# Spectral block on one core: the weights' conversion put behind the first sequence's frequency stage, rows of the forward stage asked for one chunk ahead

## Chip, cores, metric

The kernel runs on one core of one Trainium2 chip. The metric is the device time of one execution in microseconds.

## What is computed

For a batch of 8 sequences of 3136 rows of 256 numbers (float32; the two MLP matrices come as float64):

```
X  = rfft(x, axis=1)                       # along the 3136 rows
Yr = X.real @ w_r - X.imag @ w_i + b_r
Yi = X.real @ w_i + X.imag @ w_r + b_i
Yr, Yi = sign(.) * max(|.| - 0.01, 0)      # soft threshold
y  = irfft(Yr + i Yi, n=3136, axis=1)
mixed = real(fft(fft(y, axis=1), axis=2))
u  = y + mixed
un = (u - mean(u)) / sqrt(var(u) + 1e-6)   # over the 256 numbers of a row
out = u + max(un @ w_ch1, 0) @ w_ch2       # 256 -> 1024 -> 256
```

## The kernel before

The transform of length 3136 is split as 64 x 49. Each sequence b goes through stages, each a generator:

- `p1` (forward, f1): loads 12 or 13 chunks of x (`xf`), multiplies with the DFT of 64 (`g_f1`), copies the result out of PSUM (`ev`, in turn by VectorE and ScalarE, L366) and stores it in DRAM (`ad`). From b = 2 on, x is first divided into a high part `xh` (ScalarE) and a low part `xl` (GpSimd).
- `p2_f2` (frequency transform, `g_f2` from `af` and the table `tff`, L419), `p2_w` (complex weights, bias, threshold: `g_w`, `Y`), `p2_mix` (`g_mix`, `mq`, stored in DRAM as `md`), `p2_yt` and `p2_g2` (inverse, `g_g2`, stored as `bd`). The frequencies come in four quarters q.
- `p3_norm`: per norm tile of 128 rows x 2 it loads `bf` from `bd` and `mt` from `md`, makes `bh` (ScalarE) and `bl` (GpSimd, L147), multiplies (`g_g1`), adds `mt` (`ut`, L683), takes mean and variance, a square root on ScalarE, four small products on GpSimd (L695 to L698) and writes the normalised tile `nm` (L701). `p3_tr` transposes `nm` (`g_ut`, L719), `p3_mlp1` and `p3_mlp2` are the MLP (`h`, `o`).

`weights()` turns w1 and w2 from float64 (read as pairs of int32) into a high and a low float32 matrix, in 8 parts, `split_double` (L158). A part is one load of 512 KB (`raw`), one operation on ScalarE (L169), seven on VectorE (L170, L172, L174, L175, L178, L180, L182), one copy on ScalarE (L186, the high matrix) and a subtraction and an addition on GpSimd (L188, L189, the low matrix). It borrows its tiles from other stages: `raw` has the two slots of `uth`, its scratch the two slots of `mt` and the six of `ut`. In the trace its tiles are called `raw_w`, `cv_w_mt` and `cv_w_ut`.

What sets the order: each generator yields due times, `yield T * x` with T = 10000 for one sequence's worth of work; a heap takes the generator that is due first, and the instructions it writes go out in that order. Then a scheduler of the framework, which works with its own estimate of times, puts each engine's instructions in their final order. Each engine executes its own in order. All loads and stores are asked for on SyncE's queue, in order too: a request that waits holds those behind it. A tile with n slots makes the n+1st writer wait for the last reader of the first. The first sequence's frequency stage is due from 1.0 to about 1.52, sequence 1's forward stage from 1.4, the frequency stage of sequence 1 from 1.77.

Of the kernel before, what the change touches and what calls it, by code (L numbers as in the profile page):

```python
# [10 lines left out]
F32 = mybir.dt.float32  # L11
# [8 lines left out]
D = 256  # L20
# [99 lines left out]
T = 10000  # L120
# [8 lines left out]
def spectral_block(ctx: ExitStack, tc: tile.TileContext, x, w_ri, b_ri, w1, w2,  # L129
# [6 lines left out]
    sb = ctx.enter_context(tc.tile_pool(name="sb", bufs=1))  # L136
# [3 lines left out]
    def gtile(name):  # L140
        return ps.tile([128, 512], F32, tag="g", bufs=4, name=name)
# [4 lines left out]
    def lo_g(out_, full, hi):  # L146
        gp.tensor_sub(out_, full, hi.bitcast(F32))  # L147

    def mm3(o, lh, ll, rh, rl, start=True, stop=True):
        te.matmul(o, lh, rl, start=start, stop=False)  # L150
        te.matmul(o, ll, rh, start=False, stop=False)  # L151
        return te.matmul(o, lh, rh, start=False, stop=stop)  # L152
# [105 lines left out]
    def behind(key, **kw):  # L258

        assert key in af_ld  # L260
        with tc.issue_after(af_ld[key]):
            return nc.sync.dma_start(**kw)
# [7 lines left out]
    def n2_rows(t, n0, n):  # L270

        return t[n0:n0 + n].rearrange("n c u d -> (c u) n d")

    def x_rows(b, m, n):

        if m == NM - 1:
            return [xv[b + r][:, m:m + 1] for r in range(2)]
        return [xv[b][:, NM * r + m:NM * r + m + n] for r in range(2)]
# [60 lines left out]
    def p1(b):  # L339

        if b == 0:
            yield from p1_first()
            return
        for i in (b, b + 1)[:1 + (b % 2 == 0)]:
            if i not in a_dram:
                ad = dr.tile([N2, 2, U, D], F32, tag="ad", bufs=4, name=f"ad{i}")
                a_dram[i] = lambda u, ad=ad: (ad, u)
        todo = chunks + [(NM - 1, 1)] * (b % 2 == 0)
        t0, width = (1.4, 0.38) if b == 1 else (b - 0.3, 0.75)
        for ci, (m, n) in enumerate(todo):  # L350
            yield T * (t0 + width * ci / len(todo))
            w = n * D
            xf = sb.tile([128, 512], F32, tag="xf", bufs=2, name="xf")
            for r, src in enumerate(x_rows(b, m, n)):
                behind(7, out=xf[r * 64:r * 64 + 64, :w], in_=src)
            g = gtile("g_f1")
            if b == 1:
                te.matmul(g[:, :w], fwd_f, xf[:, :w], start=True, stop=True)
            else:
                xh = sb.tile([128, 512], F32R, tag="xh", bufs=1, name="xh")  # L360
                xl = sb.tile([128, 512], F32R, tag="xl", bufs=1, name="xl")
                sc.copy(xh[:, :w], xf[:, :w])  # L362
                lo_g(xl[:, :w], xf[:, :w], xh[:, :w])
                mm3(g[:, :w], *K["fwd"], xh[:, :w], xl[:, :w])
            ev = sb.tile([128, 512], F32, tag="ev", bufs=2, name="ev")
            (va.tensor_copy if ci % 2 else sc.copy)(ev[:, :w], g[:, :w])  # L366
            for r in range(2):
                ad, n2 = (a_dram[b + r](0)[0], m) if n == 1 else (a_dram[b](0)[0], NM * r + m)
                st_eng.dma_start(out=n2_rows(ad, n2, n),
                                 in_=ev[r * 64:r * 64 + 64, :w].rearrange("p (n d) -> p n d", d=D))  # L370
        done.add(("a", b))
# [390 lines left out]
    def weights():  # L762
        w1v = w1.bitcast(I32).rearrange("(k p) f -> p k f", p=128)
        w2v = w2.bitcast(I32).rearrange("(f p) e -> p f e", p=128)
        parts1 = [(np.s_[:, k, q * 512:q * 512 + 512], w1v[:, k:k + 1, q * 1024:q * 1024 + 1024])
                  for k in range(2) for q in range(2)]
        parts2 = [(np.s_[:, f:f + 2, :], w2v[:, f:f + 2]) for f in range(0, 8, 2)]
        for i, (name, shape, loads) in enumerate((("w1", [128, 2, FF], parts1), ("w2", [128, 8, D], parts2))):
            h = sb.tile(shape, F32R, tag=f"W{2 * i}", bufs=1, name=name + "h")
            l = sb.tile(shape, F32R, tag=f"W{2 * i + 1}", bufs=1, name=name + "l")  # L770
            mlp_w[name] = h, l
            for j, (sl, src) in enumerate(loads):
                yield T * (1.2 + 0.5 * (4 * i + j) / 8)
                split_double(name, h, l, sl, src)


    tasks = [load_small(), load_consts(), weights()]
    for b in range(NB):
        tasks += [f(b) for f in (p1, p2_f2, p2_w, p2_mix, p2_yt, p2_g2, p3_norm, p3_tr, p3_mlp1, p3_mlp2)]
# [44 lines left out]
```

## Time and profile before

| | |
|---|---|
| median of 3 runs | 1957.9 us (1957.82 to 1959.0) |
| profiled execution | 1958.73 us, its span 1956.9 us |
| mean granted clock of TensorE | 0.973 |
| busy share of the span | TensorE 95%, VectorE 68%, ScalarE 43%, GpSimd 36% |
| chain that ended last | TensorE 80%, DMA 6%, VectorE 6% |

PE is TensorE, DVE VectorE, ACT ScalarE, POOL GpSimd, SPq the requests on SyncE's queue. Times count from the start of the span. An engine's idle time costs something only where it is on the chain that ends last. A granted clock of 0.50 is the lower of TensorE's two levels (1.2 GHz), 1.00 the upper (2.4 GHz).

### The profile page before, as it was taken

How to read it: one execution, taken by the hardware profiler on the slowest of the kernel's cores; microseconds unless marked ns; L12 is line 12 of the kernel's file. 1: busy time of each engine (PE TensorE's matmuls, PEld its weight loads, DVE VectorE, ACT ScalarE, POOL GpSimd, SP SyncE). 2: the span in 40 equal slices, each digit the busy share in tenths (PEclk: the TensorE clock that was granted, in tenths of full speed). 3: DMA queues.
4: the chain of work that ended last, by engine and by line, in shares of the span. 5: the costliest groups of instructions: out<-in, count | busy, mean ns of one | idle time of the engine just before them, and what ended most of it. 6: DMA issues, size and time to landing. Idle time of an engine off the chain costs nothing.

```text
span 1956.9 us, 34768 instructions
## 1 busy us (share of the span) xinstructions
PE 1853.1 (95%) x12115; PEld 1703.2 (87%) x12115; DVE 1327.2 (68%) x2831; ACT 851.0 (43%) x1888; POOL 702.1 (36%) x1087
## 2 busy tenths in 40 slices
PE   4875799999999999999999999999999999999999
PEld 2764699989999999998999899998999998998999
DVE  2675687768776777766677676666777776675543
ACT  2543554445444554443544454444544434433322
POOL 0334544344333444333433442324433332322110
PEclk7986899999999999999999999999999999999999
DMA  7466554245443544335453354535443332223210
GB/s 215 123 185 193 153 137 136 90 111 142 119 133 98 157 128 123 107 102 147 132 140 105 103 153 111 139 94 153 124 118 103 94 113 87 81 70 114 63 41 25
DMA packets 163538, 233.03 MB, mean 119 GB/s; under 512 B 27484, under 2 KB 107428, under 8 KB 163364
## 3 DMA queue, kind: packets, MB, share of 16 engines
q1 hardware_dynamic: 163364, 230.82, 42.1%
q8 instruction: 96, 1.57, 0.3%
q14 instruction: 78, 0.64, 0.1%
HBM read 127.95 MB, written 102.76 MB: 118 GB/s over the span
## 4 chain that ended last, share of the span: by engine, by line
PE 80%; DMA 6%; DVE 6%; SPq 3%; issue 2%; ACT 1%; POOL 1%; DVEq 0%; POOLq 0%; ACTq 0%
PE o L151 8%; PE o L150 8%; PE o L152 8%; PE h L150 8%; PE h L152 8%; PE h L151 8%; PE g_f L419 4%; PE g_w L150 3%; PE g_w L152 3%; PE g_w L151 3%; PE g_g L150 2%; PE g_g L152 2%; PE g_g L151 2%; PE g_yt L609 2%; PE g_ut L719 2%
## 5 line engine op out<-in xcount | busy, mean ns | idle before, releaser
L151 PE MATMUL o<-w2h,hl 128*128 128x256 f32 x1568 | 431.4, 285 | 9.1 <-DVE hl L739 9.1
L739 DVE SCALAR_TENSOR_TENSOR hl<-h,hh 128x512 fp32r<-128x512 f32 (+1 forms) x416 | 272.2, 655 | 238.1 <-ACT hh L738 237.4
L738 ACT ACTIVATE hh<-h 128x512 fp32r<-128x512 f32 (+1 forms) x416 | 237.7, 572 | 435.2 <-PE h L152 379.7
L152 PE MATMUL o<-w2h,hh 128*128 128x256 f32 x1568 | 423.5, 280 | 0.0
L150 PE MATMUL o<-w2l,hh 128*128 128x256 f32 x1568 | 397.3, 286 | 5.4 <-DVE ut L758 3.5
L150 PE MATMUL h<-utl,w1h 128*128 128x512 f32 (+1 forms) x832 | 323.0, 388 | 5.8 <-DVE hl L739 5.8
L152 PE MATMUL h<-uth,w1h 128*128 128x512 f32 (+1 forms) x832 | 316.8, 381 | 0.0
L151 PE MATMUL h<-uth,w1l 128*128 128x512 f32 (+1 forms) x832 | 316.3, 380 | 0.0
L151 PEld LDWEIGHTS o<-w2h,hl 128*128 128x128 f32 x1568 | 296.5, 189 | 16.6 <-DVE hl L739 12.2
L150 PEld LDWEIGHTS o<-w2l,hh 128*128 128x128 f32 x1568 | 285.3, 189 | 18.7 <-ACT Xsh L428 3.3
L152 PEld LDWEIGHTS o<-w2h,hh 128*128 128x128 f32 x1568 | 296.5, 189 | 3.1
L147 POOL TENSOR_TENSOR bl<-bf,bh 128x512 fp32r<-128x512 f32 x104 | 129.7, 1249 | 307.4 <-ACT bh L678 304.0
L419 PE MATMUL g_f<-tff,af 98*128 98x100 f32 x1024 | 154.5, 282 | 25.6 <-DMA tff<-c_tf 12.4
L152 PEld LDWEIGHTS h<-uth,w1h 128*128 128x128 f32 x832 | 156.6, 188 | 23.8
L419 PEld LDWEIGHTS g_f<-tff,af 98*128 98x128 f32 x1024 | 147.4, 203 | 34.2 <-issue 22.7
L150 PEld LDWEIGHTS h<-utl,w1h 128*128 128x128 f32 x832 | 156.9, 189 | 20.5 <-DVE hl L739 6.6
L151 PEld LDWEIGHTS h<-uth,w1l 128*128 128x128 f32 x832 | 157.0, 189 | 13.4
L147 POOL TENSOR_TENSOR xl<-xf,xh 128x512 fp32r<-128x512 f32 (+1 forms) x75 | 97.0, 1293 | 198.9 <-ACT xh L362 197.7
L683 DVE TENSOR_TENSOR ut<-g_g,mt 128x512 f32<-128x512 f32 x104 | 68.3, 657 | 107.1 <-PE g_g L152 71.9
L147 POOL TENSOR_TENSOR Xl<-xx,Xh 128x400 fp32r<-128x400 f32 (+1 forms) x96 | 106.5, 1111 | 91.7 <-ACT Xh L428 70.5
L147 POOL TENSOR_TENSOR Xsl<-xs,Xsh 128x200 fp32r<-128x200 f32 x120 | 77.5, 647 | 155.1 <-ACT Xsh L428 140.6
L701 DVE TENSOR_SCALAR nm<-ut,ag,rs 128x256 f32<-128x256 f32 x196 | 88.6, 491 | 48.1 <-POOL rs L698 47.7
(155 smaller groups left out, 3810.5 us busy)
## 6 DMA issues: line engine op xcount, KB each, us to landing
bd<-bev SPq DMA_DIRECT2D x128, 196.0 KB
af<-ad SPq DMA_DIRECT2D x62, 392.0 KB
bf<-bd SPq DMA_DIRECT2D x184, 128.0 KB
out_dram<-ut SPq DMA_DIRECT2D x92, 256.0 KB
xf<-in_x SPq DMA_DIRECT2D x176, 128.0 KB
ad<-ev SPq DMA_DIRECT2D x168, 128.0 KB
md<-mq SPq DMA_DIRECT2D x112, 192.0 KB
mt<-md SPq DMA_DIRECT2D x416, 32.0 KB
```

What stands on the lines that cost most here:

```text
L147: gp.tensor_sub(out_, full, hi.bitcast(F32))
L150: te.matmul(o, lh, rl, start=start, stop=False)
L151: te.matmul(o, ll, rh, start=False, stop=False)
L152: return te.matmul(o, lh, rh, start=False, stop=stop)
L419: te.matmul(g[:, o:o + 100], afs[s][:, ui * D + k * 128:ui * D + k * 128 + 128], tfs[s][:, ui], start=True, stop=True)
L609: te.transpose(gt[:100, (v * 2 + o) * 128:(v * 2 + o + 1) * 128], y[:, o, place].rearrange("p c j -> p (c j)"), ident)
L683: va.tensor_add(ut[:, :n], g[:, :w].rearrange("p (n d) -> p n d", d=D), mt[:, :n])
L701: va.tensor_scalar(nm[:, j], ut[:, j], ag[:, j, 0:1], rs[:, j], op0=ALU.subtract, op1=ALU.mult)
L719: te.transpose(gv[:, k, j * 128:(j + 1) * 128], nm[:, j, k * 128:(k + 1) * 128], ident)
L738: sc.activation(hh[:, :w], h[:, :w], AF.Relu)
L739: va.scalar_tensor_tensor(hl[:, :w], h[:, :w], 0.0, hh[:, :w].bitcast(F32), op0=ALU.max, op1=ALU.subtract)
```

## The change

Three edits. The loads of a forward chunk are written out at the due time of the chunk before it (`load(ci)`), and sequence 1's forward stage is due from 1.43 over 0.35 instead of from 1.4 over 0.38. The weights' parts are due from 1.5 over 0.42 instead of from 1.2 over 0.5. A tile of 32 floats that nothing uses stands in front of w2's tiles.

```diff
@@ p1
-        t0, width = (1.4, 0.38) if b == 1 else (b - 0.3, 0.75)
+        t0, width = (1.43, 0.35) if b == 1 else (b - 0.3, 0.75)
+        xfs = {}
+
+        def load(ci):
+
+            m, n = todo[ci]
+            xfs[ci] = sb.tile([128, 512], F32, tag="xf", bufs=2, name="xf")
+            for r, src in enumerate(x_rows(b, m, n)):
+                behind(7, out=xfs[ci][r * 64:r * 64 + 64, :n * D], in_=src)
         for ci, (m, n) in enumerate(todo):
+            yield T * (t0 + width * (ci - 1) / len(todo))
+            load(ci)
             yield T * (t0 + width * ci / len(todo))
             w = n * D
-            xf = sb.tile([128, 512], F32, tag="xf", bufs=2, name="xf")
-            for r, src in enumerate(x_rows(b, m, n)):
-                behind(7, out=xf[r * 64:r * 64 + 64, :w], in_=src)
+            xf = xfs.pop(ci)
@@ weights
+            if i:
+                sb.tile([128, 32], F32, tag="pad", bufs=1, name="pad")
...
-                yield T * (1.2 + 0.5 * (4 * i + j) / 8)
+                yield T * (1.5 + 0.42 * (4 * i + j) / 8)
```

The instructions are the same in number and kind; their order differs only in the startup (up to the program places that ran at about 285 us before), but for loads of `xf` that move by a few places later on. Line numbers of the changed kernel are 8 to 10 higher. Three places follow. In these rows, [waits ...] names what the instruction waits for: DMAHW is an earlier transfer, DVE, Pool, PE and Activation are engines.

On VectorE at the last forward chunk of sequence 1 (`ev`, L366, now L374). Before, these are the last operations of part 8:

```order
L180 TENSOR_SCALAR cv_w_mt<-raw_w_1284 128x512 [waits DVE_49]
L170 TENSOR_SCALAR cv_w_mt<-cv_w_mt 128x512 [waits Activation_49]
L551 TENSOR_TENSOR mq<-g_mix,mq 100x1 [waits DMAHW1_49,DMAHW0_49,Activation_49]
L172 TENSOR_SCALAR cv_w_mt<-cv_w_mt 128x512 [waits DVE_49]
L175 TENSOR_TENSOR cv_w_ut<-cv_w_ut,cv_w_mt 128x512 [waits DVE_49]
L178 TENSOR_SCALAR cv_w_ut<-cv_w_ut 128x512 [waits DVE_49]
L551 TENSOR_TENSOR mq<-g_mix,mq 100x1 [waits Activation_49]
L182 SCALAR_TENSOR_TENSOR cv_w_ut<-cv_w_mt,cv_w_ut 128x512 [waits DVE_49]
L366 COPY ev<-g_f_1435 128x512 [waits DMAHW2_49,DMAHW3_49,DMAHW1_49,PE_49]
```

And now, of part 6 (raw tile 1414 is the second part of w2):

```order
L180 TENSOR_SCALAR cv_w_mt<-raw_w_1414 128x512 [waits DVE_49]
L172 TENSOR_SCALAR cv_w_mt<-cv_w_mt 128x512 [waits DVE_49]
L559 TENSOR_TENSOR mq<-g_mix,mq 100x1 [waits Activation_49]
L175 TENSOR_TENSOR cv_w_ut<-cv_w_ut,cv_w_mt 128x512 [waits DVE_49]
L178 TENSOR_SCALAR cv_w_ut<-cv_w_ut 128x512 [waits DVE_49]
L182 SCALAR_TENSOR_TENSOR cv_w_ut<-cv_w_mt,cv_w_ut 128x512 [waits DVE_49]
L374 COPY ev<-g_f_1382 128x512 [waits DMAHW2_49,DMAHW4_49,DMAHW1_49,DMAHW7_49,DMAHW0_49,PE_49]
```

Parts 5 to 8 stood ahead of the eviction since the last frequency product of sequence 0, now parts 1 to 6 do.

On SyncE at the `mt` loads of the first two norm tiles. Before, the end of the first tile's loads and then the second tile's:

```order
L675 DMA mt<-md_83 32x256 [waits DMAHW3_49]
L675 DMA mt<-md_83 32x256 [waits DMAHW6_49]
L673 DMA mt<-md_83 32x512
L675 DMA mt<-md_83 32x256 x2
L673 DMA mt<-md_83 32x512 [waits DMAHW0_49]
L369 DMA ad_87<-ev 64x2x256 [waits DMAHW1_49,Activation_49]
L369 DMA ad_87<-ev 64x2x256 [waits DMAHW2_49]
L675 DMA mt<-md_83 32x256 [waits DMAHW3_49]
L675 DMA mt<-md_83 32x256 [waits DMAHW4_49]
L673 DMA mt<-md_83 32x512 [waits DMAHW5_49]
L675 DMA mt<-md_83 32x256 [waits DMAHW6_49]
L675 DMA mt<-md_83 32x256 [waits DMAHW7_49]
```

Now, the second tile's, many requests further on (between the first tile's loads and these stand 19 others, among them loads of `bf`, `af` and `xf` and stores of `ad`):

```order
L677 DMA bf<-bd_84 64x2x256 [waits DMAHW7_49,Pool_49]
L262 DMA raw_w_1603<-in_w 128x2x512 [waits DMAHW0_49]
L677 DMA bf<-bd_84 64x2x256 [waits DMAHW1_49]
L681 DMA mt<-md_83 32x512 [waits DMAHW2_49,DVE_49]
L683 DMA mt<-md_83 32x256 [waits DMAHW3_49]
L683 DMA mt<-md_83 32x256 [waits DMAHW4_49]
L681 DMA mt<-md_83 32x512 [waits DMAHW5_49]
L683 DMA mt<-md_83 32x256 [waits DMAHW6_49]
L683 DMA mt<-md_83 32x256 [waits DMAHW7_49]
```

A load of `bf` (for the sixth norm tile, waiting for GpSimd's `bl` of the fourth, whose `bf` slot it takes) and the raw load of part 8 stand in front of them, and the first of them waits for VectorE.

On VectorE at the second norm tile. Before, from the first `utl` to the second tile's `nm`:

```order
L144 TENSOR_TENSOR utl<-g_ut,uth 128x2x256 [waits Activation_49]
L693 RECIPROCAL rs<-rs 128x2 [waits Activation_49]
L481 SCALAR_TENSOR_TENSOR y_1688<-g_w,bias,ks 128x400 [waits PE_49]
L481 SCALAR_TENSOR_TENSOR y_1700<-g_w,bias,ks 128x400 [waits PE_49]
L483 TENSOR_SCALAR m<-y_1688 128x400 [waits DVE_49]
L701 TENSOR_SCALAR nm<-ut,ag,rs 128x256 [waits Pool_49]
L701 TENSOR_SCALAR nm<-ut,ag,rs 128x256
L484 TENSOR_TENSOR Y<-y_1688,m 128x8x50 [waits DVE_49]
```

Now, up to the second tile's sum (`ut`, L691):

```order
L489 SCALAR_TENSOR_TENSOR y_1704<-g_w,bias,ks 128x400 [waits PE_49]
L492 TENSOR_TENSOR Y<-y_1692,m 128x8x50 [waits DVE_49]
L174 TENSOR_SCALAR cv_w_ut<-raw_w_1603 128x512 [waits DMAHW0_49]
L180 TENSOR_SCALAR cv_w_mt<-raw_w_1603 128x512
L491 TENSOR_SCALAR m<-y_1704 128x400 [waits DVE_49]
L170 TENSOR_SCALAR cv_w_mt<-cv_w_mt 128x512 [waits Activation_49]
L492 TENSOR_TENSOR Y<-y_1704,m 128x8x50 [waits DVE_49]
L172 TENSOR_SCALAR cv_w_mt<-cv_w_mt 128x512 [waits DVE_49]
L175 TENSOR_TENSOR cv_w_ut<-cv_w_ut,cv_w_mt 128x512 [waits DVE_49]
L178 TENSOR_SCALAR cv_w_ut<-cv_w_ut 128x512 [waits DVE_49]
L182 SCALAR_TENSOR_TENSOR cv_w_ut<-cv_w_mt,cv_w_ut 128x512 [waits DVE_49]
L691 TENSOR_TENSOR ut<-g_g_1651,mt 128x512 [waits DMAHW5_49,DMAHW6_49,DMAHW4_49,DMAHW7_49,DMAHW3_49,DMAHW2_49]
```

Part 8's seven operations stand in front of the second tile's sum. Part 7's stand in the same way in front of and among the first tile's, with L188 and L189 on GpSimd among the four small products.

## Rows read from the trace of the kernel before

**Rows 1.** The table of windows; columns: stretch in us, its length, then busy us (and instructions) of PE, PEld, DVE, ACT and POOL, granted clock, busy share of the DMA engines, GB/s.

```profile
150.00:200.00 50.00, 25.51 (x89) 19.23 (x88) 26.24 (x38) 18.04 (x39) 26.96 (x22) 0.60 0.65 183
...
250.00:300.00 50.00, 50.00 (x338) 46.44 (x337) 40.74 (x86) 24.05 (x54) 24.23 (x33) 1.00 0.50 134
...
300.00:431.00 131.00, 125.42 (x835) 115.04 (x833) 101.39 (x199) 60.22 (x135) 51.87 (x70) 1.00 0.38 108
...
431.00:1957.00 1526.00, 1505.67 (x10130) 1402.21 (x10130) 1038.77 (x2266) 661.41 (x1449) 533.45 (x866) 1.00 0.40 111
```

**Rows 2.** The timeline of TensorE, 82 to 206 us: the rows that waited; columns: start, duration, engine, line, operation, output<-inputs, shapes, how many, and in brackets the wait in front of it and who ended it.

```profile
97.39 1.09 PE L609 MATMUL g_yt<-ident,Y 128*100 128x128 f32 x4 [3.79 <-ACT bev L640]
...
109.53 1.10 PE L358 MATMUL g_f<-xf,fwd_f 128*128 128x512 f32 x2 [0.90 <-DVE cv_w_ut L174]
...
112.11 0.68 PE L538 MATMUL g_mix<-csf,ef 128*100 128x129 f32 x4 [1.49 <-ACT bev L640]
...
114.16 0.70 PE L150 MATMUL g_w<-Xl,wdh 128*128 128x400 f32 x1 [1.36 <-DVE Xl L144]
...
135.93 2.04 PE L358 MATMUL g_f<-xf,fwd_f 128*128 128x512 f32 x2 [3.26 <-issue]
```

**Rows 3.** The table of windows for TensorE alone, four stretches; columns: stretch, length, busy us (instructions), granted clock, DMA share, GB/s.

```profile
96.90:103.70 6.80, 6.31 (x21) 0.50 0.57 183
114.00:117.40 3.40, 3.24 (x9) 0.50 0.59 159
134.50:139.90 5.40, 3.97 (x10) 0.50 0.51 155
205.30:209.50 4.20, 4.18 (x12) 0.50 0.72 182
```

**Rows 4.** The conversion's instructions by their scratch tile, the whole execution; columns: line, engine, operation, tiles, how many, duration in ns (least/median/most), first and last start.

```profile
L174 DVE TENSOR_SCALAR cv_w_ut<-raw_w x8: 411/771/1493, 85.7 to 163.2; 128x512 int32<-128x512 int32 x8
...
L178 DVE TENSOR_SCALAR cv_w_ut<-cv_w_ut x8: 414/423/2272, 89.6 to 166.6; 128x512 int32<-128x512 int32 x8
...
L182 DVE SCALAR_TENSOR_TENSOR cv_w_ut<-cv_w_mt,cv_w_ut x8: 679/693/1699, 93.2 to 167.0; 128x512 f32<-128x512 int32 x8
...
L188 POOL TENSOR_TENSOR cv_w_ut<-cv_w_ut,w1h x4: 1272/1366/1494, 91.6 to 115.3; 128x512 f32<-128x512 f32 x4
...
L189 POOL TENSOR_TENSOR w1l<-cv_w_ut x4: 1312/1320/1389, 94.0 to 118.0; 128x512 fp32r<-128x512 f32 x4
```

**Rows 5.** The timeline of VectorE at parts 5 to 8 and the last forward eviction of sequence 1.

```profile
144.63 1.23 DVE L174 TENSOR_SCALAR cv_w_ut<-raw_w 128x512 int32<-128x512 int32 x1 [0.18 <-DMA raw_w<-in_w]
...
155.97 0.69 DVE L182 SCALAR_TENSOR_TENSOR cv_w_ut<-cv_w_mt,cv_w_ut 128x512 f32<-128x512 int32 x1
...
161.60 1.64 DVE L182 SCALAR_TENSOR_TENSOR cv_w_ut<-cv_w_mt,cv_w_ut 128x512 f32<-128x512 int32 x1
...
163.17 0.41 DVE L174 TENSOR_SCALAR cv_w_ut<-raw_w 128x512 int32<-128x512 int32 x1
...
165.85 0.69 DVE L175 TENSOR_TENSOR cv_w_ut<-cv_w_ut,cv_w_mt 128x512 int32<-128x512 int32 x1
...
167.04 0.69 DVE L182 SCALAR_TENSOR_TENSOR cv_w_ut<-cv_w_mt,cv_w_ut 128x512 f32<-128x512 int32 x1
...
167.65 0.68 DVE L366 COPY ev<-g_f 128x512 f32<-128x512 f32 x1
```

**Rows 6.** The timeline of SyncE's queue: the raw loads of parts 5 and 6, the first `mt` load of the first and of the second norm tile, a `bf` load; the second column is how long the request took to issue.

```profile
139.86 1.55 SPq L262 DMA_DIRECT2D raw_w<-in_w  x2
...
195.00 0.33 SPq L673 DMA_DIRECT2D mt<-md  x1
...
197.69 0.42 SPq L673 DMA_DIRECT2D mt<-md  x1
...
218.21 0.61 SPq L669 DMA_DIRECT2D bf<-bd  x1
```

**Rows 7.** The timeline of TensorE: first frequency product of sequence 1, first `g_ut`, last product of the second norm tile, second `g_ut`.

```profile
176.30 1.15 PE L419 MATMUL g_f<-tff,af 98*128 98x100 f32 x4 [3.33 <-DMA af<-ad]
...
205.32 0.66 PE L719 MATMUL g_ut<-ident,nm 128*128 128x128 f32 x2 [9.60 <-DVE nm L701]
...
207.92 0.63 PE L152 MATMUL g_g<-bh,invh 128*128 128x512 f32 x1
...
214.07 0.41 PE L719 MATMUL g_ut<-ident,nm 128*128 128x128 f32 x2 [1.42 <-ACT bh L678]
```

**Rows 8.** The timelines of VectorE, ScalarE and GpSimd at the first norm tiles: the two sums, the table load for the square root, a `bh` and a `bl`.

```profile
199.24 0.69 DVE L683 TENSOR_TENSOR ut<-g_g,mt 128x512 f32<-128x512 f32 x1 [11.83 <-DMA mt<-md]
...
208.58 0.69 DVE L683 TENSOR_TENSOR ut<-g_g,mt 128x512 f32<-128x512 f32 x1 [0.59 <-DMA af<-ad]
...
201.22 1.28 ACT L691 ACT_TABLE_LOAD   x1
...
213.44 0.62 ACT L678 CAST bh<-bf 128x512 fp32r<-128x512 f32 x1 [2.09 <-DMA bf<-bd]
...
214.14 1.74 POOL L147 TENSOR_TENSOR bl<-bf,bh 128x512 fp32r<-128x512 f32 x1 [1.01 <-ACT bh L678]
```

**Rows 9.** Groups of instructions from the page: the MLP's second product; columns: how many | busy us, mean ns | idle before and who ended it.

```profile
L151 PE MATMUL o<-w2h,hl 128*128 128x256 f32 x1568 | 431.4, 285 | 9.1 <-DVE hl L739 9.1
...
L150 PE MATMUL o<-w2l,hh 128*128 128x256 f32 x1568 | 397.3, 286 | 5.4 <-DVE ut L758 3.5
```

## The prediction

> **What bounds the kernel now.** I read the table of windows first. From 250 us to the end TensorE is busy 50.00 of 50, 125.42 of 131 and 1505.67 of 1526 us [rows 1]: 1681.1 of 1707, so that only 25.9 us are idle there. What happens after 250 us is a queue of matmuls in a fixed order, and a start that is d later ends d later. The 40 slices of the page say the same. The time to be won or lost lies before 250 us: between 150 and 200 TensorE is busy 25.51 of 50, at a granted clock of 0.60, while VectorE has 26.24 and GpSimd 26.96 [rows 1]. No engine is full there; TensorE follows a chain of dependent steps.
>
> The rows of TensorE's waits say which chains. Between 97 and 117 it waits four times for work that stands beside the weights' conversion: 3.79, 0.90, 1.49 and 1.36 us [rows 2], 7.54 together; behind two of these waits the clock is at 0.50, the lower level of 1.2 GHz, for 6.80 and 3.40 us [rows 3]. At 135.93 it waits 3.26 us before a first forward matmul [rows 2]. The next chain is that of the first norm tile: sequence 1's frequency transform (`g_f` from `tff` and `af`) starts at 176.30, the first transposition of a normalised tile (`g_ut`) at 205.32 after 9.60 us of waiting, the second tile's `g_ut` at 214.07 after 1.42 [rows 7]. TensorE executes in order, so what stands behind these two `g_ut` (the MLP among it) cannot pass them.
>
> **The change, part by part.**
>
> *Parts 1 to 4 leave the first frequency stage.* Gone from there are 4 x 10 instructions and their waits. The 7.54 us of waits go, and the 10.2 us at half clock would take 5.1: 12.6. The rows of the sequence-1 chunk asked one chunk ahead can also take the 3.26 us at 135.93, as its queue row no longer stands behind the use of the chunk before. I take 15.9; bounds 12.6, and 18.6 with the half clock of 134.5 to 139.9 (2.7 us) gone too [rows 2, 3]. The first raw part now waits for the last frequency product of sequence 0, as parts 5 and 6 did, which were asked for at 139.86 [rows 6]: it is asked for at about 124.0.
>
> *Six parts in place of four before the last forward chunk.* In the order, the last forward eviction of sequence 1 stands on VectorE behind the last operation of part 6; in the kernel before, behind that of part 8, but only parts 5 to 8 were left to do then. From the request to the first operation it took 4.8 us (139.86 to 144.63) [rows 5, 6], so part 1 starts at 128.8. Four parts took from 144.63 to 167.73, 5.8 us each [rows 5]; single ones 6.6 (156.66 to 163.24) and 4.5 (163.24 to 167.73). Six at 5.8 are 34.7: to 163.5. From the last operation to `g_f` of sequence 1 it is 167.65 to 176.30, 8.65 us (eviction, store, load) [rows 5, 7]: 172.2 in place of 176.30, **4.1 us earlier**. So the 15.9 won are nearly used up by two more parts (11.6). Bounds: 14.3 earlier (18.6 won and 4.5 a part: 121.3 + 4.8 + 27.0 + 8.65 = 161.7), 4.6 later (12.6 won and 6.6 a part).
>
> Why 5.8 and not the operations' own 3.4 (five of 0.41 and two of 0.69 at best): a `tensor_scalar` of the conversion takes 0.41 us at best and up to 1.49 or 2.27 [rows 4], and the long ones lie beside GpSimd's two subtractions and additions of 1.3 us. The Trainium skill (SBUF — State Buffer, section "SBUF: two separate sides") says that VectorE and GpSimd take a shared port pair in turn as an exclusive lock, for the whole instruction; the trace agrees as far as the stretched rows go. By that rule taken alone, with no overlap at all, a part would be an estimated 3.4 + 2.7 = 6.1, six parts 36.6, and the end 1.9 us later than I forecast; the sum above goes by the rows.
>
> *Part 7 inside the first norm tile.* Its L174, L180 and L175 stand on VectorE between the tile's sum and its variance, L188 and L189 on GpSimd before and between the four small products. 0.41 + 0.41 + 0.69 and one GpSimd row of 1.3 [rows 4] make 2.8; L178, L182 and the other GpSimd row lie beside the 1.28 us of the square root's table load [rows 8]. Bounds: 0, and 5.2 if nothing overlaps. The first `g_ut` comes at 205.3 - 4.1 + 2.8 = 204.0, and the end of the first `g_g` product of the second tile (208.55 before [rows 7]) at 207.3, 1.3 earlier.
>
> *Part 8 in front of the second norm tile.* This is the term that decides. The queue on SyncE holds, in order: a `bf` load that waits for GpSimd's `bl` of the fourth tile; raw part 8; then the second tile's `mt` loads, which wait for L175 of part 8, since part 8's scratch has the `mt` slots. Before, those loads were asked for at 197.69, directly behind the first tile's (195.00), with nothing to wait for [rows 6], and the second tile's sum came at 208.58, when its product was done [rows 8]. Now, from the product's end: `bh` 0.62 and `bl` 1.5 (that row is 1.74, the 128x512 ones around 1.26) [rows 8], the `bf` issue 0.61 [rows 6], raw 4.8, from L174 to the end of L175 3.0 (163.17 to 166.54 is 3.4 with L180 stretched to 1.52) [rows 5], `mt` from request to sum 4.24 (195.00 to 199.24) [rows 6, 8]: 14.8 us, where it was 0. From the sum to `g_ut` it took 5.49 (208.58 to 214.07) with other work on ScalarE and VectorE in the way; I allow 1.0 less. So the second `g_ut` comes **13.8 later relative to the product**. What hid it was the early request for `mt`; that cover is gone. TensorE has only 4.1 us of products left to run meanwhile (208.55 to the start of the 1.42 us wait before 214.07). Bounds: 12 and 16.
>
> *The clock behind it.* After the 9.60 us wait the clock stood at 0.50 for 4.20 us [rows 3], which costs 2.1. A wait of 15 us more would bring this once more; I take 1.5, bounds 0 and 2.1.
>
> *Rows one chunk ahead in the other sequences.* After the startup the order of the queue moves by two to four places per sequence, that of the other engines not at all; 25.9 us idle bound a gain, and they would have to be waits for these rows. Nothing; bounds 0 and -4.
>
> *The pad* gives `w2h` and some small tiles other addresses in SBUF. The products that read `w2h` and those that read `w2l`, from two places, take 285 and 286 ns [rows 9]: nothing; no row bounds it otherwise.
>
> Sum against the profiled execution (1958.73, span 1956.9 and 1.8 around it): -4.1 + 2.8 + 13.8 + 1.5 = +14.0, 1972.7. The median of the runs is 0.8 lower than the profiled one, so I predict **1972**.
>
> **Rivals.**
>
> *The gain carries and cancels the loss (1954 to 1962).* In 150 to 200 VectorE and GpSimd are idle half the time [rows 1], so the conversion could run in round trips of DMA. With 4.5 us a part the chain is 14.3 earlier, and -14.3 + 2.8 + 13.8 + 0 = +2.3, 1961. For it: one part did run in 4.5. Against it: the three before it took 18.6 (144.63 to 163.24) [rows 5].
>
> *Faster (1940 to 1954).* The same, and part 8's chain is found shorter or is covered: if raw part 8 is fetched while `bl` of the fourth tile is early (its data are in time), the loss falls from 13.8 to 6 and part 7 costs nothing: -14.3 + 6 = -8.3, 1950. It decides at a loss in the second tile below the gain in the first. Against it: the `bl` needs the slot that the second tile's product frees, whatever its data do.
>
> *Slower still (1982 and more).* Parts at 6.6, part 7 not overlapped, two dips of the clock: +4.6 + 5.2 + 16 + 2.1 = +27.9, 1986.
>
> *The change doesn't reach the end:* the waits after 250 us absorb it. They sum to 25.9 us in 1707 and come from each sequence's own chain, so I give this no time of its own; it is in the second case of cancelling.
>
> **How the numbers follow.** Forecast (1962 to 1982) 0.60, cancelling 0.18, faster 0.16, slower still 0.06. A run of this kernel tells no change from one below 0.2%, 3.9 us. Slower by more: 0.60 + 0.06 and little of the cancelling, 0.67; within: 0.16; faster: 0.17. The range leaves out 0.06 above 1982 and about 0.12 below 1953.
>
> **What would show it.** Right: no waits on conversion between 85 and 125; raw part 1 asked for at 122 to 127; `g_f` of sequence 1 between 170 and 176; the second norm tile's `mt` loads asked for some 10 us behind the first's and a TensorE wait of 12 us or more in front of the second `g_ut` and the MLP and the end as much later. Wrong: parts at 4.5 us or less, a second `g_ut` before 216, or a queue that lets the `mt` loads go ahead of part 8.

## The result, and the profile after

The changed kernel takes 1977.33 us (median of four runs, 1970.95 to 1980.86), the kernel before beside it 1957.86 (1956.98 to 1959.0): a ratio of 1.0085, 95% interval 1.0065 to 1.0105, so slower by 19.5 us. The profiled execution took 1980.86, 22.1 more than that of before (1958.73).

The table of windows of the changed kernel, with the columns of [rows 1] (the last three stretches reach to the end):

```profile
150.00:200.00 50.00, 26.54 (x90) 19.14 (x90) 31.07 (x42) 17.49 (x37) 24.18 (x20) 0.63 0.66 187
200.00:250.00 50.00, 25.06 (x120) 22.58 (x121) 27.44 (x62) 17.76 (x38) 24.32 (x36) 0.69 0.44 113
250.00:300.00 50.00, 50.00 (x342) 46.41 (x340) 42.01 (x86) 27.41 (x60) 25.88 (x32) 1.00 0.50 139
300.00:450.00 150.00, 144.98 (x970) 133.47 (x968) 112.47 (x224) 67.47 (x151) 57.83 (x82) 1.00 0.40 111
450.00:1979.00 1529.00, 1506.67 (x10131) 1402.55 (x10130) 1039.22 (x2272) 662.57 (x1452) 535.34 (x868) 1.00 0.39 111
```

From 250 us on TensorE is as full as in [rows 1]: 27.4 of 1729 us idle, before 25.9 of 1707. The stretch 200 to 250 is where the time is missing: TensorE is busy 25.06 of 50, and VectorE and GpSimd about half, so again a chain and no full engine. TensorE's waits (start, duration, engine, line, operation, tiles; in brackets the wait in front and who ended it), to be read against [rows 7]:

```profile
128.69 2.05 PE L366 MATMUL g_f<-xf,fwd_f 128*128 128x512 f32 x2 [3.17 <-DMA xf<-in_x]
...
152.93 2.05 PE L366 MATMUL g_f<-xf,fwd_f 128*128 128x512 f32 x2 [17.44 <-DMA xf<-in_x]
...
180.25 1.15 PE L427 MATMUL g_f<-tff,af 98*128 98x100 f32 x4 [7.76 <-DMA af<-ad]
...
211.65 0.66 PE L727 MATMUL g_ut<-ident,nm 128*128 128x128 f32 x2 [13.69 <-DVE nm L709]
...
232.90 0.66 PE L727 MATMUL g_ut<-ident,nm 128*128 128x128 f32 x2 [13.28 <-DVE nm L709]
```

All waits on the conversion between 85 and 125 are gone. The second norm tile, which TensorE entered after a wait of 1.42 us [rows 7], now makes it wait 13.28. SyncE's queue of the changed kernel shows why (columns as in [rows 6]):

```profile
131.77 1.06 SPq L262 DMA_DIRECT2D raw_w<-in_w  x2
...
147.56 0.36 SPq L262 DMA_DIRECT2D raw_w<-in_w  x1
147.97 2.10 SPq L262 DMA_DIRECT2D xf<-in_x  x3
...
197.64 0.32 SPq L681 DMA_DIRECT2D mt<-md  x1
...
216.98 0.61 SPq L677 DMA_DIRECT2D bf<-bd  x1
217.63 0.60 SPq L262 DMA_DIRECT2D raw_w<-in_w  x1
218.28 0.61 SPq L677 DMA_DIRECT2D bf<-bd  x1
224.78 0.32 SPq L681 DMA_DIRECT2D mt<-md  x1
```

The second tile's `mt` loads go out at 224.78, 27.1 us behind the first tile's (197.64); before, 2.7 us behind [rows 6]. They went out when VectorE had done L175 of part 8, as VectorE's rows of the changed kernel show (part 1's first operation, part 6's last with the eviction behind it, the first tile's sum, part 8's L174 and L175, the second tile's sum):

```profile
136.90 1.51 DVE L174 TENSOR_SCALAR cv_w_ut<-raw_w 128x512 int32<-128x512 int32 x1 [1.12 <-DMA raw_w<-in_w]
...
170.72 0.69 DVE L182 SCALAR_TENSOR_TENSOR cv_w_ut<-cv_w_mt,cv_w_ut 128x512 f32<-128x512 int32 x1
171.32 0.68 DVE L374 COPY ev<-g_f 128x512 f32<-128x512 f32 x1
...
201.80 0.69 DVE L691 TENSOR_TENSOR ut<-g_g,mt 128x512 f32<-128x512 f32 x1 [7.22 <-DMA mt<-md]
...
221.82 0.43 DVE L174 TENSOR_SCALAR cv_w_ut<-raw_w 128x512 int32<-128x512 int32 x1 [1.06 <-DMA raw_w<-in_w]
...
224.06 0.69 DVE L175 TENSOR_TENSOR cv_w_ut<-cv_w_ut,cv_w_mt 128x512 int32<-128x512 int32 x1
...
228.90 0.69 DVE L691 TENSOR_TENSOR ut<-g_g,mt 128x512 f32<-128x512 f32 x1 [2.96 <-DMA mt<-md]
```

The last row bears two readings. The sum stands behind all seven operations of part 8, which ended at 225.9, and it then waited 2.96 us more for its `mt` rows.

The whole difference can be put into one sum, stage by stage, in the two profiled executions. `g_f` of sequence 1: 180.25 against 176.30, +3.95. From there to the first tile's sum: 21.55 against 22.94, -1.4. From the sum to the first `g_ut`: 9.85 against 6.08, +3.8. From the first `g_ut` to the second: 21.25 against 8.75, +12.5. From there to the first product of the MLP (`h`): 8.34 (to 241.24) against 6.48 (to 220.55), +1.9. Together +20.7. From the first `h` to TensorE's last product it is 1733.8 against 1732.4, +1.4. That makes the 22.1.

### The profile page after: what moved, and what is told of

It reads as the page before. It is cut to its first block, busy times and chain, and to the rows that moved or that the text cites. A ratio compares the mean times of both kernels' runs of the same rounds, so it can differ in the third digit from the quotient of the medians.

```text
span 1979.0 us, 34764 instructions
## 1 busy us (share of the span) xinstructions
PE 1851.7 (94%) x12115; PEld 1703.9 (86%) x12115; DVE 1324.3 (67%) x2831; ACT 852.3 (43%) x1888; POOL 703.4 (36%) x1087
## 4 chain that ended last, share of the span: by engine, by line
PE 78%; DMA 7%; DVE 7%; SPq 3%; issue 2%; POOL 1%; ACT 1%; DVEq 0%; POOLq 0%; ACTq 0%
PE o L151 8%; PE o L150 8%; PE o L152 8%; PE h L150 8%; PE h L151 8%; PE h L152 8%; PE g_f L427 4%; PE g_w L150 3%; PE g_w L152 3%; PE g_w L151 3%; PE g_yt L617 2%; PE g_g L150 2%; PE g_g L151 2%; PE g_g L152 2%; PE g_ut L727 2%
## 5 line engine op out<-in xcount | busy, mean ns | idle before, releaser
L151 PE MATMUL o<-w2h,hl 128*128 128x256 f32 x1568 | 430.7, 284 | 10.3 <-DVE hl L747 10.3
L691 DVE TENSOR_TENSOR ut<-g_g,mt 128x512 f32<-128x512 f32 x104 | 68.3, 657 | 103.1 <-PE g_g L152 68.4
```

The source lines that it names most:

```text
L691: va.tensor_add(ut[:, :n], g[:, :w].rearrange("p (n d) -> p n d", d=D), mt[:, :n])
```

## The experiments

Each kernel was timed beside runs of the kernel before on the same chip. The table gives its ratio to them with the 95% interval, and five places of its profile in us: raw part 1 (or, where parts 1 to 4 had their old place, part 5) asked for, `g_f` of sequence 1, from the first norm tile's sum to the first `g_ut` with the number of parts converted in between, from the first to the second `g_ut`, and the first `h`.

| kernel | ratio | raw | g_f | sum to g_ut (parts) | g_ut to g_ut | first h |
|---|---|---|---|---|---|---|
| before (its profile) | | 139.9 | 176.3 | 6.1 (0) | 8.8 | 220.6 |
| changed | 1.0085 [1.0065, 1.0105] | 131.8 | 180.3 | 9.9 (1) | 21.3 | 241.2 |
| changed, again | 1.0072 [1.0050, 1.0094] | 129.7 | 178.0 | 10.1 (1) | 21.4 | 239.5 |
| weights_only | 1.0055 [1.0035, 1.0075] | 123.6 | 164.5 | 11.0 (1) | 20.8 | 225.3 |
| rows_only | 1.0026 [1.0011, 1.0042] | 135.6 | 179.2 | 6.3 (0) | 7.4 | 221.7 |
| p8_early | 1.0041 [1.0023, 1.0059] | 127.6 | 177.4 | 14.2 (2) | 8.0 | 227.8 |
| p78_early | 0.9996 [0.9980, 1.0013] | 128.3 | 177.5 | 6.5 (0) | 7.5 | 223.0 |
| own_mt | 1.0048 [1.0031, 1.0066] | 129.0 | 178.0 | 8.7 (1) | 18.0 | 232.4 |
| no_pad | 1.0116 [1.0098, 1.0134] | 130.4 | 179.3 | 10.1 (1) | 21.1 | 240.1 |
| b_pad | 1.0038 [1.0024, 1.0052] | 138.2 | 174.4 | 6.5 (0) | 8.8 | 220.4 |
| w_p78 | 1.0025 [1.0013, 1.0038] | 123.5 | 167.5 | 5.9 (0) | 10.3 | 218.6 |
| w_p78_pad | 0.9989 [0.9978, 0.9999] | 124.4 | 170.3 | 5.9 (0) | 10.2 | 219.8 |
| w_pad | 1.0021 [1.0002, 1.0041] | 127.3 | 169.7 | 10.7 (1) | 20.5 | 230.5 |
| w_p8_pad | 0.9988 [0.9974, 1.0003] | 123.7 | 167.4 | 14.5 (2) | 8.3 | 218.5 |

Runs of one kernel spread by up to 8 us either way of their median on the chip of the experiments, the kernel before too (35 runs, 1952.72 to 1969.41), so the ratios are to be read with their intervals, and the places of the profile carry the argument.

**Which of the two edits costs the time?** First the moved weights alone, in the kernel before, without the rows edit and without the pad:

```
-                yield T * (1.2 + 0.5 * (4 * i + j) / 8)
+                yield T * (1.5 + 0.42 * (4 * i + j) / 8)
```

> The kernel before with the weights' due times alone (1.5 over 0.42). In its order parts 1 to 6 stand before the last forward chunk, part 7 in the first norm tile and raw part 8 in front of the second tile's mt loads, as in the changed kernel. Theory (the place of parts 7 and 8 costs the time): second g_ut at 227 to 235 us, 12 us or more of TensorE waiting in front of it, time 1970 to 1982. Rival 1 (the rows asked one chunk ahead, or the shorter forward stage, cost it): time within 4 us of the kernel before. It also shows whether the first raw part, asked for at 131.8 where 124.0 was forecast, is late because of the rows edit: then it is asked for at about 124 here; if the first frequency stage simply gains less than its waits sum to, at 130 or later.

Measured: 1972.02, ratio 1.0055, inside the expected time; the second `g_ut`, expected at 227 to 235, came at 216.98. TensorE's waits of this kernel:

```profile
164.52 1.15 PE L419 MATMUL g_f<-tff,af 98*128 98x100 f32 x4 [3.21 <-DMA af<-ad]
...
196.18 0.66 PE L719 MATMUL g_ut<-ident,nm 128*128 128x128 f32 x2 [13.76 <-DVE nm L701]
...
216.98 0.66 PE L719 MATMUL g_ut<-ident,nm 128*128 128x128 f32 x2 [13.07 <-DVE nm L701]
```

Raw part 1 was asked for at 123.57, 16.3 before part 5 of the kernel before, and `g_f` came 11.8 earlier than in [rows 7]. The second `g_ut` is 2.9 later than there, with the same wait of 13 us as in the changed kernel. So the loss in front of the second tile belongs to the moved weights. The rest, that `g_f` of the changed kernel is 15.7 later than here, goes with the rows edit, though starts differ by up to 5 us between two profiles of the same order (`g_f` at 164.5 here, at 169.7 in w_pad). The edit alone (the changed kernel with the old due times of the weights and without the pad) has two halves, the loads a chunk ahead and the later due time of sequence 1's forward stage; no run separates them:

```
-                yield T * (1.5 + 0.42 * (4 * i + j) / 8)
+                yield T * (1.2 + 0.5 * (4 * i + j) / 8)
-            if i:
-                sb.tile([128, 32], F32, tag="pad", bufs=1, name="pad")
```

> The changed kernel with the weights' due times of before (1.2 over 0.5) and no pad, so the rows asked one chunk ahead and the due times of sequence 1's forward stage alone. Theory: the first norm tiles come as before (second g_ut at 210 to 218 us), time 1954 to 1962. Rival 1 (this edit costs the time): 1968 or more. A gain of the 3.26 us wait before a forward matmul at 136 us would show as 1954 to 1955.

Measured: 1966.62, ratio 1.0026, where 1954 to 1962 was expected. The first `h` is 1.2 later than before (221.7); from there to TensorE's last product it is 1740.0 in place of 1732.4. Of these 7.6 us up to 6.8 are clock: in that stretch the granted clock stood at 0.50 for 20.4 us, before for 6.8, and half of the difference is what it can cost. Whether the edit brings that is not shown (the other profiles with the edit and the pad have 3.4 to 10.2 us of it), so that part of the ratio stays open. By itself the edit wins nothing at the start, and it costs some 10 us at `g_f` when the weights stand where the change puts them: 177.4 to 180.3 in the six runs with both (median 178.0), 164.5 to 170.3 in the five with the moved weights alone (median 167.5).

**Are parts 7 and 8 the loss in the norm tiles?** Part 8 due together with part 7, all else as changed; then both due with part 6:

```
-                yield T * (1.5 + 0.42 * (4 * i + j) / 8)
+                yield T * (1.5 + 0.42 * min(4 * i + j, 6) / 8)
```

> The changed kernel with one number different: part 8 is due together with part 7. Its raw load stands behind that of part 7 in the queue, and its vector operations in front of the first tile's nm. Theory (raw part 8 and the mt loads behind it cost 12 us): the first g_ut comes 3 to 4 later (215), the second g_ut about 7 to 9 after it (222 to 224 where it was 232.9), time 8 to 11 below the changed kernel, 1965 to 1969. Rival 2 (the conversion costs by the engines' time, wherever it stands): no change beyond 3 us, since the same operations stand in the same stretch.

```
-                yield T * (1.5 + 0.42 * (4 * i + j) / 8)
+                yield T * (1.5 + 0.42 * min(4 * i + j, 5) / 8)
```

> The changed kernel with parts 7 and 8 due together with part 6. In the order both stand between the last forward evictions and the first norm tile's sum, where VectorE was idle for 10.8 us in the changed kernel, and the second tile's mt loads stand right behind the first's. Theory: first forward chunk and g_f of sequence 1 as in the changed kernel (180), first g_ut 3 to 4 earlier than there (208), second g_ut about 9 behind it (216 to 218), time 1958 to 1963, 14 to 18 below the changed kernel. Rival 2 (the engines' time): at most 5 below it.

Measured: 1968.9 and 1960.33, ratios 1.0041 and 0.9996, both within the expected times. The two `g_ut` of the second of them:

```profile
209.25 0.66 PE L727 MATMUL g_ut<-ident,nm 128*128 128x128 f32 x2 [12.88 <-DVE nm L709]
...
216.70 0.41 PE L727 MATMUL g_ut<-ident,nm 128*128 128x128 f32 x2 [0.68 <-DVE nm L709]
```

The wait in front of the second tile falls from 13.28 to 0.68 and the second `g_ut` comes 16.2 earlier, with the same eight parts. With part 8 beside the first tile (p8_early) the wait of the second is gone as well, but the first tile takes 14.2 from sum to `g_ut`. Over the whole table that stretch is 5.9 to 6.5 with no part in it, 8.7 to 11.0 with one, 14.2 and 14.5 with two: about 4 us a part.

The change was also repeated.

> The changed kernel once more, beside the others of this call. The startup's landmarks should repeat to about 4 us: first raw part asked for at 128 to 132, second g_ut 21 us behind the first, first MLP product at 237 to 242, and the stretch from there to the end should vary by the stretches at half clock alone (1732 to 1740 us so far). Time 10 to 20 above the kernel before of the same call.

Measured: 1977.39, ratio 1.0072, with the same two waits (13.53 and 14.80 us in front of the two `g_ut`).

**Is it the scratch in the `mt` slots?** The conversion's two `mt` tiles put into other slots (tag `hh`, not in use yet at that time), so that the second tile's loads need not wait for L175 of part 8:

```
-        tf = tmp("mt", 2, F32)
-        r = tmp("mt", 2)
+        tf = tmp("hh", 2, F32)
+        r = tmp("hh", 2)
```

> The changed kernel with the conversion's scratch in the two slots of hh (idle until the MLP) in place of the two of mt. Then the second tile's mt loads stand right behind the first's and wait for no conversion, but raw part 8 stays behind the bf load, and part 8's vector operations stay in front of the second tile's sum. Theory (bl, bf and raw part 8 are three quarters of the chain, the mt slot the rest): the second g_ut comes 2 to 5 us nearer to the first than in the changed kernel (17 to 19 in place of 21), time 2 to 5 below it. Rival (the mt slots are the cause): 10 or more below it, second g_ut 9 to 11 behind the first.

Measured: 1972.03, ratio 1.0048, 5.4 below the repeat (2 to 5 were expected). From `g_ut` to `g_ut` it is 18.0 in place of 21.3:

```profile
206.64 0.66 PE L727 MATMUL g_ut<-ident,nm 128*128 128x128 f32 x2 [9.93 <-DVE nm L709]
...
224.64 0.66 PE L727 MATMUL g_ut<-ident,nm 128*128 128x128 f32 x2 [10.92 <-DVE nm L709]
```

So the slots are 3.3 of the 12.5 us, about the 2.96 that the sum waited for `mt` in the changed kernel. What is left is not the `mt` loads. In this kernel they stand right behind the first tile's and go out at 196.48, 14.8 us ahead of raw part 8. SyncE's row of the first of them and the row of raw part 8, then VectorE's first and last operation of part 8 and the second tile's sum:

```profile
196.48 0.43 SPq L681 DMA_DIRECT2D mt<-md  x1
...
211.28 0.59 SPq L262 DMA_DIRECT2D raw_w<-in_w  x1
...
215.70 0.43 DVE L174 TENSOR_SCALAR cv_w_ut<-raw_w 128x512 int32<-128x512 int32 x1 [1.03 <-DMA raw_w<-in_w]
...
219.47 0.69 DVE L182 SCALAR_TENSOR_TENSOR cv_w_ut<-cv_w_hh,cv_w_ut 128x512 f32<-128x512 int32 x1
220.08 0.68 DVE L691 TENSOR_TENSOR ut<-g_g,mt 128x512 f32<-128x512 f32 x1
```

The sum waits for nothing of its own; it stands on VectorE behind part 8, and part 8 waits for its raw load. That load stands here behind a store of `ad` (209.34) that waits for the eviction at 208.62 of a forward product issued behind the first `g_ut`; no `bf` load that waits for GpSimd is in front of it, though the expectation had one there. So 9.2 of the 12.5 us belong to the order on VectorE (and to part 8's last row on GpSimd, which ends at 222.66 in front of the small products) together with the late raw load.

**Is the pad free?** The changed kernel without its pad, the order of all instructions the same:

> The changed kernel without the 32 floats in front of w2's tiles; the order of every engine is the same. Theory: the pad moves addresses and costs nothing, so within 3 us of the changed kernel of the same call, and its landmarks are those. Rival: the addresses of w2's tiles matter for the products that read them; then the mean of the 128x256 products moves from 280 to 286 ns and the time by 10 us or more either way.

Measured: 1985.45, ratio 1.0116, 8 us more than the repeat with the pad (1977.39), where at most 3 was expected. The pad's only effect is on addresses; it puts `w2h` and `w2l` 128 bytes further, and with them the tiles laid out behind them (`xh`, `xl`, `bf`, `nm` and smaller ones). The groups of the page that read `w2h`, first of the changed kernel, then without the pad (columns as in [rows 9]):

```profile
L151 PE MATMUL o<-w2h,hl 128*128 128x256 f32 x1568 | 430.7, 284 | 10.3 <-DVE hl L747 10.3
...
L152 PE MATMUL o<-w2h,hh 128*128 128x256 f32 x1568 | 423.2, 279 | 0.0
```

```profile
L151 PE MATMUL o<-w2h,hl 128*128 128x256 f32 x1568 | 434.2, 286 | 7.9 <-DVE hl L747 7.9
...
L152 PE MATMUL o<-w2h,hh 128*128 128x256 f32 x1568 | 426.9, 281 | 0.0
```

Each takes 2 ns more on the mean. From the first `h` to the end TensorE is busy 1721.4 us without the pad, 1710.4 and 1708.5 with it. As a test by itself, the kernel before with nothing but the pad, which shifts its `w2h` by the same 128 bytes, out of the place it had:

```
+            if i:
+                sb.tile([128, 32], F32, tag="pad", bufs=1, name="pad")
             h = sb.tile(shape, F32R, tag=f"W{2 * i}", bufs=1, name=name + "h")
```

> The kernel before with only the pad ahead of the w2 tiles: same order of instructions, w2h and w2l 128 bytes further in SBUF. Theory (the place of w2h in steps of 128 bytes decides the pace of the products that read it, as the runs with and without the pad differ): the first h stays at 220 to 221, the products from w2h take 281 to 282 ns and those from w2l 286 in place of 279 and 284, TensorE is busy some 8 us longer behind the first h, and the time is 1.003 to 1.005 of before. Rival (the slower products of the runs without the pad come with the moved weights, or from run to run): 279 and 284 ns, within 0.2% of before.

Measured: 1966.93 beside 1960.75, ratio 1.0038: slower by 6.2 us with the order unchanged.

```profile
L151 PE MATMUL o<-w2h,hl 128*128 128x256 f32 x1568 | 434.6, 286 | 11.1 <-DVE hl L739 11.1
...
L152 PE MATMUL o<-w2h,hh 128*128 128x256 f32 x1568 | 427.0, 281 | 0.0
```

The first `h` stands at 220.4 as before, and behind it TensorE is busy 1722.1 in place of 1710.3. Up to 5 of these 11.8 us are clock (17.0 us at 0.50 behind the first `h` in place of 6.8), and the means of the groups hold such stretches too. Outside them the traces part cleanly: by the start times, from a product that reads `w2h` to the next product it is a median of 118 ns in the four kernels with `w2h` on the two slow places (no_pad, b_pad, weights_only, w_p78), and 115 to 116 in the other ten. From before to b_pad that comes to about 6.5 us over the 3 x 1568 products that read w2, the size of the 6.2. So the cost goes with the place of w2's tiles, and the pad in the change puts them back on a good one after the moved weights had shifted them: taken by itself the pad makes the changed kernel faster, and the kernel before slower.

**Is there a better place for the parts?** The moved weights without the rows edit, parts 7 and 8 due with part 6, first without the pad, then with it; then the moved weights with the pad as they are, and with part 8 due with part 7. The due times are the lines shown above.

> The kernel before with the weights' due times of the change, parts 7 and 8 due together with part 6, rows not asked ahead, no pad. Theory (moving the conversion out of the first frequency stage wins about 16 us, the rows edit takes some 5 to 8 of them away, parts 7 and 8 in the norm chain the rest): first raw part at 124, g_f of sequence 1 at 164 to 166, first g_ut at 193 to 196, second at 202 to 205, time 8 to 12 below the kernel before. Rival 2 (the conversion costs by the engines' time wherever it stands): g_f at 174 or later and no gain. Rival 3 (parts 7 and 8 are not covered in front of the first tile): first g_ut at 200 or later, gain under 5.

> The kernel before with the moved weights, parts 7 and 8 due with part 6, and the pad. Theory: as the run of the same order without the pad up to the first h (218 to 219), and 8 us less behind it: a ratio of 0.998 to 0.999 against 1.0025 without the pad. Rival (no address effect): 1.0025 again.

> The kernel before with the moved weights and the pad, rows not asked for ahead. Theory (order and address add): first h at 225 as in the run with the moved weights alone, products from w2h at 279 ns, so some 8 us less than that run behind the first h: before + 4 to + 6, a ratio of 1.002 to 1.003. Rival (no address effect): 1.0055 as that run.

> The kernel before with the moved weights, part 8 due with part 7 (both behind the first norm tile's load, ahead of the second's), and the pad; rows not asked for ahead. Theory: the first frequency stage gives back its 16 us (raw part 1 asked for at 123 to 125), six parts cost 35, the second norm tile's loads stand behind no part any more: first g_ut at 198 to 200 (two parts beside it), second g_ut at 206 to 208, first h at 213 to 215, 6 to 7 us earlier than before, products at the pace of before: 1953 to 1956 where before is 1961, a ratio of 0.996 to 0.998. Rival (VectorE's and GpSimd's time for the eight parts has to be paid ahead of the first h wherever they stand): first h at 218 or later, ratio 0.999 or more.

Measured: 1966.1 (1.0025), 1957.1 (0.9989), 1966.23 (1.0021) and 1956.56 (0.9988). The pad is worth 0.36% between the first two and 0.34% between weights_only and w_pad, each against the kernel before beside it, some 7 us. In w_pad the time came as expected, but the first `h`, expected at 225, at 230.5. The first of the four missed what was expected, 1949 to 1953, and came as its third rival said: its first `g_ut` came at 201.8, not at 193 to 196. The wait only moved to the step ahead of the norm, where GpSimd had two more parts to do (its last row of part 8 ended at 178.25):

```profile
186.31 0.80 PE L150 MATMUL g_g<-bl,invh 128*128 128x512 f32 x1 [12.62 <-POOL bl L147]
```

The last missed too: first `h` expected at 213 to 215, measured 218.5.

```profile
167.41 1.15 PE L419 MATMUL g_f<-tff,af 98*128 98x100 f32 x4 [5.13 <-DMA af<-ad]
...
203.69 0.66 PE L719 MATMUL g_ut<-ident,nm 128*128 128x128 f32 x2 [16.57 <-DVE nm L701]
211.94 0.41 PE L719 MATMUL g_ut<-ident,nm 128*128 128x128 f32 x2 [1.42 <-DVE nm L701]
```

`g_f` is 8.9 earlier than before, and 8.4 of it go into the two parts beside the first tile (14.5 against 6.1). The rival, that the time of the eight parts is paid ahead of the first `h` wherever they stand, named 218 or later and came closer here. Against p78_early it does not hold as a rule, where the same work was 18.3 us cheaper at the first `h` (223.0 against 241.2) than in the changed kernel. What the runs bear out lies between: a part on the chain whose raw load has been fetched in time costs some 4 us, and one whose raw load is asked for late, ahead of the second tile's sum, costs 12.5. Both best versions are about 0.1% faster than the kernel before, hardly more than the intervals can tell.

## Why the prediction was right, and where not

**The sign and the size.** 1972 was forecast, 1977.33 measured, inside the range. The step that was to decide did. Two of the signs named for a right forecast did not show: raw part 1 asked for at 122 to 127 (131.8) and `g_f` between 170 and 176 (180.25). The range of 10 us either way held all the same: the error of 8.0 at `g_f` went through to the end, less 1.3 at part 8 and 1.4 on the way to the first tile's sum. By its own terms the bounds of `g_f` are 14.6 earlier and 4.0 later, not 14.3 and 4.6; the measured 3.95 later lies at the edge.

**Part 8.** Forecast +13.8 with bounds of 12 and 16, measured +12.5 between the two `g_ut`; p8_early and p78_early take it away. The chain ran as the rows said, `bh`, `bl`, `bf`, raw part 8, L175, `mt`, sum: 14.0 us from the end of the second tile's product (214.88) to its sum (228.90), forecast 14.8. Two of its links are not shown to be needed. The `bf` load waited for `bl` until 216.92, but a store of `ad` and two `xf` loads in front of it held the queue until 216.89, and in own_mt raw part 8 is nearly as late behind the first `g_ut` without such a `bf` load (4.6 us, here 6.0). And with the `mt` slots free 9.2 us stay, since the sum stands behind part 8 on VectorE as well: the early `mt` request was not the only cover that part 8 took away.

**Six parts before the last forward chunk.** Forecast 34.7 us, 5.8 each; 34.5 from the first operation (136.90) to the end of part 6 (171.41), 5.75 each. From the request to the first operation 5.1 against 4.8, from the last operation to `g_f` 8.85 against 8.65. These steps of the sum held; in all eleven profiles with the moved weights the six parts took 34.5 to 35.5. The Trainium skill (SBUF — State Buffer, section "SBUF: two separate sides") lets VectorE and GpSimd use their shared ports only in turn; taken alone it gave an estimated 6.1 a part. The measured 5.75 lies below that, so the trace agrees in part: operations of VectorE of 0.41 us alone take 1.48 to 1.52 in many places between 136 and 171.

**Where the sum began.** Raw part 1 was put at 124.0 and came at 131.8 (129.7 in the repeat). This is the mis-sized term, 7.8 us; it carries `g_f` to 180.25 in place of 172.2 and turns the 4.1 us gain into a loss of 3.95. The moved weights alone reach 123.57, close to the forecast, but in part by luck: the wait of 3.26 that the sum took away is still there (3.24 us in front of the forward matmul at 121.00), so 16.3 us were won where the other terms make 12.6, or 15.3 with the half clock of 134.5 to 139.9 [rows 3] gone as well, as it is in this profile (granted clock 1.00 from 121 to 125.5). The failed step is to credit the rows edit with the 3.26 us in front of the first forward matmul [rows 2]. In its place stand waits for the same rows, 2.47 and 3.17 us in front of the forward matmuls at 104.23 and 128.69 of the changed kernel. Half the delay stands already at the last frequency product of sequence 0, 100.73 against 96.94 in w_p8_pad; runs with the edit and the moved weights have the `g_f` group of this stage that waits for a load of `tff` (in w_pad a store of `bd`) at 83.8 to 86.4, those with the weights alone at 80.5 to 83.8. What sets that first half is open.

**What the forecast did not see of the rows edit.** With it, the `xf` rows of the next chunk stand on SyncE behind raw part 4 (147.56, then 147.97), which has to wait for a raw slot (VectorE's last reading of part 2 is an L180 at 147.07). They end the 17.44 us wait of TensorE at 152.93; raw part 4's own wait is 2.2 us of it (145.38 to 147.56). That this wait moved `g_f` is not shown, since VectorE works through parts 1 to 6 without a gap meanwhile. The order on VectorE is the other thing: it has the forward eviction for which `g_f` waits behind part 6 (171.32), in all six kernels with the edit and the moved weights. Without the edit, in all five, it stands ahead of the last operation of part 5, as in w_p8_pad, in VectorE's rows:

```profile
155.48 0.68 DVE L366 COPY ev<-g_f 128x512 f32<-128x512 f32 x1
156.08 1.56 DVE L182 SCALAR_TENSOR_TENSOR cv_w_ut<-cv_w_mt,cv_w_ut 128x512 f32<-128x512 int32 x1
...
162.48 0.69 DVE L182 SCALAR_TENSOR_TENSOR cv_w_ut<-cv_w_mt,cv_w_ut 128x512 f32<-128x512 int32 x1
```

There `g_f` comes 4.2 us behind the end of part 6 (163.17 to 167.41), with the edit 8.85; over all of them it is 2.0 to 5.9 without the edit and 8.4 to 9.4 with it. That 4.6 and the later start (5.6 between the medians, 129.3 and 123.7) make nearly all of the 10.5 between the medians of `g_f`. The forecast had the place of the eviction right for the changed kernel, but did not ask which of the two edits put it there, and so priced the rows edit at a gain.

**Part 7.** Forecast +2.8, bounds 0 and 5.2; measured +3.8. The forecast hid one of GpSimd's two rows beside the table load; GpSimd's rows of the changed kernel show both between the variance and `rs`. VectorE's `rs` was ready at 208.07, so L188 held the first of the four small products (L703) for 0.9 us and L189 the second (L704) for its whole 1.25:

```profile
207.73 1.25 POOL L188 TENSOR_TENSOR cv_w_ut<-cv_w_ut,w2h 128x512 f32<-128x512 f32 x1
208.94 0.19 POOL L703 TENSOR_TENSOR vv<-vv,rs 128x2 f32<-128x2 f32 x1
209.09 1.25 POOL L189 TENSOR_TENSOR w2l<-cv_w_ut 128x512 fp32r<-128x512 f32 x1
...
210.86 0.20 POOL L706 TENSOR_TENSOR rs<-rs,vv 128x2 f32<-128x2 f32 x1
```

**The clock term** of 1.5 stands in the 1.9 from the second `g_ut` to the first `h`: behind that wait the granted clock was 0.50 for 4.8 us. **Rows ahead in the other sequences**: nothing measurable, 1.4 behind the first `h` in all.

**The pad.** "Nothing" was right for the changed kernel, whose products take 284 and 286 ns against 285 and 286 in [rows 9], but for the wrong reason: comparing `w2h` with `w2l` said nothing on other places. This is luck: without the pad the same change took 1985 (no_pad), outside the range.

**The rivals.** "Cancels" needed parts of 4.5 us; they took 5.75. "Faster" needed a cheap part 8; it cost 12.5.

## What to carry to other kernels

Before moving work out of a stage, list in every queue, the DMA queue and each engine's own, what will stand right behind it at the new place: here one part whose load came late, ahead of one sum and of that sum's six loads, cost 12.5 us, most of the 16.3 that leaving the old place had won. When a change has two edits, price each by itself in the order that it makes, since the one that looks harmless (rows asked for earlier) can push back an eviction on which the next stage waits. Where two versions differ by less than 1%, compare the time of the same instruction group first, outside the stretches at half clock: what the shift of a tile in memory costs can be as large as what the change does.

## What the runs showed of the hardware that was not expected

The pace of TensorE's products went with the place in SBUF of the tile that they read: with w2's tiles 128 bytes further the kernel took 6.2 us more in b_pad, and with them 128 bytes nearer 8 more in no_pad. The profile page's means for the products of 128x256 that read `w2h` are 281 and 286 ns in both, 279 and 284 in the changed kernel (280 and 285 before); outside the stretches at half clock the start of the next product follows after a median of 118 ns in place of 115 to 116. In the built programs `w2h` of the changed kernel lies 3328 bytes behind that of before, 13 times 256, and the two run alike; the slow places, no_pad and b_pad, lie 128 bytes beside these. Whether it is `w2h` or `w2l` was not separated, no other places were tried, and the products that read `w1h`, which did not move, were about 1 ns slower with them. The mechanism was not tried.
